# Splitting a weight unit over three chunks of time, and copying out the second accumulator ahead of the rounding

## The chip, the cores and the metric

The kernel runs on one core of a Trainium2 chip. Its time is the device time of one execution in microseconds (us). TensorE (PE in the profile; PEld is its weight load) multiplies matrices into PSUM, VectorE (DVE) and ScalarE (ACT) work elementwise on SBUF and PSUM, GpSimd (POOL) works on SBUF alone, and SyncE (SP) issues the transfers. Each engine runs its own queue in order; what crosses engines is ordered by semaphores.

## The reference

A 7-tap convolution with weights made from a softmax at every token, and two two-layer networks one after the other, on 8192 tokens of 192 values with 2048 hidden values:

```python
w = softmax(weight_gen)                     # per token and head, over 7 taps
x = einsum('bshk,bskhg->bshg', w, x_unf)    # x_unf: the last 7 tokens, 8 heads of 24
h = x @ w_in                                # 192 -> 2048
g = where(h > 0, h, exp(minimum(h, 0)) - 1)
x = g @ w_out                               # 2048 -> 192
h = x @ w_in2
g = h * clip(h + 3, 0, 6) / 6
out = g @ w_out2
```

## The kernel before

**Precision.** TensorE takes rounded 32-bit operands (F32R) at its fast rate. To come near full precision, every operand of a product is kept as a high part (rounded) and a low part (the rest), and a product is three matmuls: high by high, high by low, low by high. So x is split into `xh` and `xl`, g into `gh` and `gl`, and each weight into `_h` and `_l` tiles.

**Blocks, chunks, units.** The tokens come in 16 blocks of 512 (`NB`). A *chunk* is one block with 256 of the 2048 hidden values: 18 matmuls to make h (`first_product`, two halves k of 64 partitions that run as pairs, in the banks h), the nonlinearity, and, three chunks later (`LAG`), 20 matmuls of g with `w_out` (`second_product`) into two accumulators, `acca` and `accb`. In the order of the list `cells`, chunks 0 to 15 (`BOOT`, `EARLY`) serve blocks 0 and 1 with the first network's weights as they arrive, five slices of block 0, five of block 1, and the rest; from chunk 16 each block takes 8 chunks in a row, 128 chunks for each network. A *unit* is a slice of 384 columns of a weight (`w_in` or `w_out`) that has to be split into its parts. Units 0 to 15 are the first network's; chunk d needs its unit split before it starts.

**Splitting a unit.** It is loaded as 64-bit words (`raw`). ScalarE takes an absolute value (L150), VectorE does five steps (`s0` to `s4`: L154, L157, L161, L169, L178), ScalarE casts the high part (L171, queued in `s3`, and ready to run when L161 is done). For units 0 to 15, TensorE then adds up the low part in PSUM (`p5`: L183 to L185, the "low product"), and ScalarE casts it out (`p6`: L190, the "low cast"). The working tile of the five steps is a PSUM bank for units flagged `busy`, and the SBUF tile `bootf` for the others.

**The order.** It is written out by hand. In chunk n, TensorE gets `matmuls(n)` and then the low product of the unit whose steps were queued at the end of chunk n-1 (`at[u] == n - 1`). ScalarE and VectorE get `act_a` and `gate` of half 1 and of half 0 (two activations, L487 and L488, and the VectorE operation L504, the "gate"), the low cast, then `round_g` (ScalarE casts gh of chunk n-1, L494, the "rounding") and `rest_g` (VectorE makes gl, L498). At the chunk's end ScalarE's absolute value and VectorE's five steps of the next unit are queued, with ScalarE's high cast. From chunk 16 on, the rounding stands between the two halves of activations.

**Around it.** GpSimd makes the convolution's products of a block (L278 to L299); they wait for the softmax weights (VectorE, L268) and for the tile `y`, of which there is one. `prepare` transposes y on TensorE (L323, L327), casts `xh` on ScalarE (L334), makes `xl` on VectorE (L336) and moves halves of both by transfers, which for blocks 1 and 2 wait for the next chunk (`later(1, ...)`). When a block's last second product is done, `fold_b` copies `accb` to SBUF (L359), or, for blocks 0 and 1, whose sums were begun earlier, adds the kept part to it on VectorE (L357); a chunk later `fold_a` copies `acca`, and ScalarE (L364) and VectorE (L366) put the two together as z. The next block's first matmul into `accb` waits for this.

Of the kernel before, what the change touches and what calls it, by code (L numbers as in the profile page):

```python
# [17 lines left out]
def kernel(  # L18
# [105 lines left out]
    class Unit:  # L124
# [39 lines left out]
        def s3(self):  # L164
            if self.m == 0 and self.busy:
                self.r = self.b
            else:
                self.r = stage.tile([P, UN], U32, tag="tr", name="tr", bufs=2)
            nc.vector.tensor_scalar(self.r, self.f, 0xFF800000, None, op0=ALU.bitwise_and)  # L169
            hi, _, v = self.parts()  # L170
            nc.scalar.copy(hi, v(self.f.bitcast(F32)))  # L171
# [139 lines left out]
    def prepare(m, i, parts=(0, 1)):  # L311
# [20 lines left out]
        def split():  # L332
# [6 lines left out]
            for k in "hl":  # L339
                for a in range(2):  # L340
                    later(1 if first[m, i] <= BOOT else 2, X[k][half[1 - a], 1].bitcast(F32), X[k][half[a], 0].bitcast(F32))
# [7 lines left out]
    def fold_b(m, i):  # L349
# [6 lines left out]
        if (m, i) in part:  # L356
            nc.vector.tensor_tensor(b, accb, part.pop((m, i)), op=ALU.add)  # L357
        else:
            nc.scalar.copy(b, accb)  # L359
        bv, zb = b.rearrange("p (h t c) -> p h t c", h=2, c=HP), v[:, :, TM:]  # L360

        def rest():
            for k in range(2):
                nc.scalar.copy(zb[half[k]], bv[half[1 - k], :, 2 * k:2 * k + 2])  # L364
# [207 lines left out]

    at = []
    for d, *_ in units:
        at.append(min(d - 2, at[-1] + 1) if at else -2)
# [8 lines left out]
    def want(n):  # L584
        if n < len(units) and n not in made:
            u = made[n] = Unit(*units[n])
            u.n = n
            if n < BOOT:
                u.busy = at[n] < 3 or at[n] > 7
# [16 lines left out]
    begin = {i: max(8, prep[0, i - 1] + (i == 3)) for i in range(2, NB)}  # L606
# [4 lines left out]
    with tc.manual_schedule():  # L611
# [11 lines left out]
        for s in todo["a"] + todo["w"]:  # L623
            s()
        made[0].p5()
# [5 lines left out]
        for s in c1[4:] + w_steps(1):  # L631
            s()
        wst = Stream(wtasks)
        for n in range(len(cells) + LAG + 3):
            now = n
            jobs = []
            for m, i in order:
# [4 lines left out]
                elif (m, i) == (0, 2) and 0 <= n - prep[m, i] < 2:  # L642
                    jobs.append(prepare(m, i, (n - prep[m, i],)))
# [3 lines left out]
            low = [made[u] for u in range(BOOT) if at[u] == n - 1]  # L647
            for u in low:
                u.p5()

            for k in (1, 0):
                if n < len(cells):
                    act_a(n, k)
                    gate(n, k)
                if not k:
                    for u in low:
                        u.p6()
                if k == (n >= BOOT) and 1 <= n <= len(cells):
                    round_g(n - 1)
                    rest_g(n - 1)  # L660
                if not k:
                    continue
                if n - LAG in (SPLIT - 1, 2 * SPLIT - 1):
                    keep_b(*ends[n - LAG])
                for b in order:
                    if n == last[b] + LAG:
                        fold_b(*b)
# [55 lines left out]
```

## Time and profile before

| | |
|---|---|
| median of 3 runs | 1295.91 us (1294.05 to 1296.14) |
| profiled execution | 1292.77 us, span 1291.0 us |
| TensorE busy | 1215.9 us (94%) |
| VectorE busy | 940.5 us (73%) |
| ScalarE busy | 852.5 us (66%) |
| GpSimd busy | 411.1 us (32%) |

A share of busy time is an average over stretches with different limits. The kernel has a first part, in which weights and x arrive and are split while chunks 0 to 15 run, and a long even part. The profile's views used here give busy time by stretch with the granted TensorE clock (1.00 is 2.4 GHz, and the other level is half of it), who waited for whom, and the instructions of an engine in order of time, with the idle time ahead of one and what ended it in brackets.

### The profile page before, as it was taken

Reading aid. Unit: us, or ns where it says so; the run is one execution under the profiler, and the core shown is the slowest. Engines: PE = TensorE matmul, PEld = TensorE weight load, DVE = VectorE, ACT = ScalarE, POOL = GpSimd, SP = SyncE. Lnnn points to the kernel's source line nnn. Section 1 sums busy time; section 2 is a strip of 40 time slices with the busy share of each in tenths; the row PEclk is TensorE's granted clock in tenths of the full one; section 3 lists DMA queues with packets and bytes.
Section 4 is the critical chain, followed back from the end, with each engine's and each line's share of the span. In section 5 each row is a group of like instructions: output and inputs, shape, how many; then the busy total and the mean of one; then the engine's idle time right before and its main releaser. Section 6 shows DMA issues by size and latency. Waiting matters only on the chain.

```text
span 1291.0 us, 25448 instructions
## 1 busy us (share of the span) xinstructions
PE 1215.9 (94%) x10176; PEld 1093.0 (85%) x10176; DVE 940.5 (73%) x1226; ACT 852.5 (66%) x1340; POOL 411.1 (32%) x234
## 2 busy tenths in 40 slices
PE   3777779999999999999999999999999999999998
PEld 2555658888888988888887799999999999999996
DVE  5778478898888988988876766666666666666663
ACT  2554457788878887888887556665555665656653
POOL 7434258766666887666500000000000000000000
PEclk9888889999999999999999999999999999999999
DMA  6231112222112222221121111111111111111110
GB/s 175 74 108 37 48 50 84 84 85 66 53 50 84 84 85 84 80 66 36 38 62 50 38 51 50 36 34 44 50 50 51 43 45 50 50 32 31 50 39 25
DMA packets 33686, 75.82 MB, mean 59 GB/s; under 512 B 4644, under 2 KB 17058, under 8 KB 33568
## 3 DMA queue, kind: packets, MB, share of 16 engines
q1 hardware_dynamic: 33568, 74.19, 19.8%
q8 instruction: 80, 1.31, 0.4%
q14 instruction: 38, 0.31, 0.1%
HBM read 36.43 MB, written 12.58 MB: 38 GB/s over the span
## 4 chain that ended last, share of the span: by engine, by line
PE 67%; ACT 15%; DVE 13%; issue 3%; DMA 1%; SPq 0%; DVEq 0%; ACTq 0%
PE h L467 30%; PE acca L467 21%; PE accb L467 14%; DVE gl L498 5%; ACT gh L494 4%; ACT r L487 4%; ACT r L488 4%; DVE r L504 2%; DMA xl<-xl 1%; DVE tr L169 1%; DVE bootf L161 1%; DVE wt L243 1%; DVE aux L157 1%; DMA xt<-in_x_dram 1%; ACT fold L359 0%
## 5 line engine op out<-in xcount | busy, mean ns | idle before, releaser
L467 PE MATMUL h<-xh,wi_h 64*128 64x512 f32 x1536 | 581.8, 400 | 5.0 <-DVE xl L336 2.6
L467 PE MATMUL h<-xh,wi_l 64*128 64x512 f32 x1536 | 583.6, 400 | 0.1
L467 PE MATMUL h<-xl,wi_h 64*128 64x512 f32 x1536 | 573.5, 397 | 2.7 <-DMA xl<-xl 2.0
L498 DVE TENSOR_TENSOR gl<-r,gh 128x1024 fp32r<-128x1024 f32 x256 | 372.6, 1456 | 64.3 <-ACT gh L494 63.0
L490 ACT ACTIVATE r<-h,three 128x512 f32<-128x512 f32 x256 | 176.2, 688 | 229.9 <-PE h L467 117.0
L467 PEld LDWEIGHTS h<-xh,wi_h 64*128 64x128 f32 x1536 | 288.6, 188 | 19.9 <-DMA xh<-xh 3.1
L507 DVE SCALAR_TENSOR_TENSOR r<-r,h 128x512 f32<-128x512 f32 x256 | 176.0, 688 | 173.9 <-ACT r L490 173.1
L467 PEld LDWEIGHTS h<-xl,wi_h 64*128 64x128 f32 x1536 | 285.7, 187 | 17.8 <-DMA xl<-xl 3.0
L467 PEld LDWEIGHTS h<-xh,wi_l 64*128 64x128 f32 x1536 | 285.6, 187 | 14.7 <-ACT wi_l L190 0.9
L467 PE MATMUL acca<-gh,wo 64*128 64x512 f32 x1024 | 286.7, 400 | 0.0
L494 ACT CAST gh<-r 128x1024 fp32r<-128x1024 f32 x256 | 265.9, 1039 | 2.1 <-DVE r L504 1.3
L504 DVE SCALAR_TENSOR_TENSOR r<-r,h 128x512 f32<-128x512 f32 x256 | 174.4, 682 | 84.4 <-ACT r L488 84.0
L467 PEld LDWEIGHTS acca<-gh,wo 64*128 64x128 f32 x1024 | 193.7, 189 | 15.3
L487 ACT ACTIVATE r<-h 128x512 f32<-128x512 f32 x256 | 152.5, 596 | 79.1 <-PE h L467 48.6
L278 POOL TENSOR_TENSOR tmp<-xt,wt 128x768 f32<-128x768 f32 (+1 forms) x96 | 190.0, 1979 | 7.0 <-DMA xt<-in_x_dram 0.8
L467 PE MATMUL accb<-gh,wo 64*128 64x512 f32 x512 | 170.8, 414 | 15.5 <-ACT fold L359 6.0
L488 ACT ACTIVATE r<-r 128x512 f32<-128x512 f32 x256 | 162.0, 633 | 8.1
L467 PE MATMUL accb<-gl,wo 64*128 64x512 f32 x512 | 165.9, 404 | 0.0
L467 PE MATMUL acca<-gl,wo 64*128 64x512 f32 x512 | 163.2, 399 | 0.0
L285 POOL TENSOR_TENSOR y<-y,tmp 128x768 f32<-128x768 f32 (+1 forms) x80 | 146.6, 1832 | 6.3
L467 PE MATMUL acca<-gh,wo1b 64*128 64x512 f32 x512 | 140.9, 394 | 0.3
L467 PE MATMUL acca<-gh,wo1a 64*128 64x512 f32 x512 | 140.3, 393 | 0.0
(143 smaller groups left out, 1850.4 us busy)
## 6 DMA issues: line engine op xcount, KB each, us to landing
xt<-in_x_dram SPq DMA_DIRECT2D x14, 960.0 KB, 5.4
xh<-xh SPq DMA_DIRECT2D x64, 192.0 KB, 2.7
xl<-xl SPq DMA_DIRECT2D x64, 192.0 KB, 2.9
raw<-in_moe_w_out_dram SPq DMA_DIRECT2D x16, 384.0 KB, 3.2
z<-z SPq DMA_DIRECT2D x16, 384.0 KB, 2.3
zin<-z SPq DMA_DIRECT2D x16, 384.0 KB, 3.0
out_dram<-ot SPq DMA_DIRECT2D x16, 384.0 KB, 2.3
raw<-in_moe_w_in_dram SPq DMA_DIRECT2D x16, 192.0 KB, 3.4
```

The source lines that it names most:

```text
L157: nc.vector.tensor_scalar(self.b, self.b, 3, 0x3FFFFFF8, op0=ALU.logical_shift_left, op1=ALU.bitwise_and)
L161: nc.vector.scalar_tensor_tensor(self.f, self.hw, 0xC0000000, self.b, op0=ALU.bitwise_and, op1=ALU.bitwise_or)
L278: eng.tensor_tensor(o.rearrange("p t (h g) -> p t h g", g=G), xk, wk.rearrange("p (t h) g -> p t h g", h=H), op=ALU.mult)
L285: eng.tensor_tensor(y[:, t, :], y[:, t, :], o, op=ALU.add)
L467: mm = nc.tensor.matmul(o, w, r, start=st, stop=sp).ins
L487: nc.scalar.activation(r, h, AF.Relu, scale=-1.0)
L488: nc.scalar.activation(r, r, AF.Exp, scale=-1.0)
L490: nc.scalar.activation(r, h, AF.Relu, bias=three)
L494: nc.scalar.copy(gg[n][0], rs[n])
L498: nc.vector.tensor_tensor(gl, rs.pop(n), gh.bitcast(F32), op=ALU.subtract)
L504: nc.vector.scalar_tensor_tensor(r, r, -1.0, h, op0=ALU.add, op1=ALU.max)
L507: nc.vector.scalar_tensor_tensor(r, r, 6.0, h, op0=ALU.min, op1=ALU.mult)
```

## The change

Units 0 to 15 have their stages apart. In chunk n, TensorE does the low product of the unit whose five steps were queued at the end of chunk n-2, and ScalarE its low cast; the high cast, now a function of its own (`high`), is queued at the start of chunk n for the unit of chunk n-1. All units are begun one chunk earlier (`d - 3` for `d - 2`), and unit 2 before chunk 0. `busy` is now set for units 0 to 5 alone, so units 6 to 15 do their five steps in SBUF; before, that were units 7 to 11. For chunks before 16, rounding and `rest_g` of chunk n-1 come at the start of chunk n, ahead of the activations. Block 2 is begun one chunk later (`max(9, ...)`), its two transposes stand ahead of the chunk's activations (`early`), and its transfers go out in the same chunk. From chunk 16 on, the copy of the second accumulator stands ahead of the rounding; for blocks 0 and 1 it is a copy on ScalarE too, and the kept part is added a chunk later on VectorE, from SBUF.

```diff
             nc.vector.tensor_scalar(self.r, self.f, 0xFF800000, None, op0=ALU.bitwise_and)
+            if self.m:
+                self.high()
+
+        def high(self):
             hi, _, v = self.parts()
             nc.scalar.copy(hi, v(self.f.bitcast(F32)))
...
-                    later(1 if first[m, i] <= BOOT else 2, X[k][half[1 - a], 1].bitcast(F32), X[k][half[a], 0].bitcast(F32))
+                    later(first[m, i] == SPLIT if first[m, i] <= BOOT else 2, X[k][half[1 - a], 1].bitcast(F32), X[k][half[a], 0].bitcast(F32))
...
         if (m, i) in part:
-            nc.vector.tensor_tensor(b, accb, part.pop((m, i)), op=ALU.add)
-        else:
-            nc.scalar.copy(b, accb)
+            first_part = part.pop((m, i))
+        else:
+            first_part = None
+        nc.scalar.copy(b, accb)
...
         def rest():
+            if first_part is not None:
+                nc.vector.tensor_tensor(b, b, first_part, op=ALU.add)
...
-        at.append(min(d - 2, at[-1] + 1) if at else -2)
+        at.append(min(d - 3, at[-1] + 1) if at else -3)
...
-                u.busy = at[n] < 3 or at[n] > 7
+                u.busy = n < 6
...
-    begin = {i: max(8, prep[0, i - 1] + (i == 3)) for i in range(2, NB)}
+    begin = {i: max(9, prep[0, i - 1] + (i == 3)) for i in range(2, NB)}
...
+        made[1].high()
+        for s in w_steps(2):
+            s()
...
-                    jobs.append(prepare(m, i, (n - prep[m, i],)))
+                    early = prepare(m, i, (n - prep[m, i],))
...
-            low = [made[u] for u in range(BOOT) if at[u] == n - 1]
+            low = [made[u] for u in range(BOOT) if at[u] == n - 2]
             for u in low:
                 u.p5()
+            if early:
+                early()
+            if 1 <= n < BOOT:
+                round_g(n - 1)
+                rest_g(n - 1)
+            for u in range(BOOT):
+                if at[u] == n - 1:
+                    made[u].high()
...
+                if k:
+                    if n - LAG in (SPLIT - 1, 2 * SPLIT - 1):
+                        keep_b(*ends[n - LAG])
+                    for b in order:
+                        if n == last[b] + LAG:
+                            fold_b(*b)
+                if k and BOOT <= n <= len(cells):
+                    round_g(n - 1)
+                    rest_g(n - 1)
                 if not k:
                     for u in low:
                         u.p6()
-                if k == (n >= BOOT) and 1 <= n <= len(cells):
-                    round_g(n - 1)
-                    rest_g(n - 1)
```

Where this puts things shows in the queues. On ScalarE, chunk 6 before: absolute value (L150) and high cast (L171) of unit 9, the activations, unit 9's low casts (L190, a `w_out` unit has two), and the rounding of chunk 5's g (L494).

```order
L150 ACTIVATE bootf<-raw 128x384
L171 CAST wo_88<-bootf 128x2x192
L487 ACTIVATE r<-h_73 128x512
L488 ACTIVATE r<-r 128x512
L487 ACTIVATE r<-h_72 128x512
L488 ACTIVATE r<-r 128x512
L190 CAST wo_88<-aux 128x2x128
L190 CAST wo_88<-aux 128x2x64
L494 CAST gh<-r 128x1024
```

The same chunk on ScalarE in the changed kernel, whose line numbers are 4 to 7 higher (L175, L194, L494, L495 and L501 are the operations above):

```order
L150 ACTIVATE bootf<-raw 128x384
L501 CAST gh<-r 128x1024
L175 CAST wi_h<-bootf 128x384
L494 ACTIVATE r<-h_73 128x512
L495 ACTIVATE r<-r 128x512
L494 ACTIVATE r<-h_72 128x512
L495 ACTIVATE r<-r 128x512
L194 CAST wo_88<-aux 128x2x128
L194 CAST wo_88<-aux 128x2x64
```

The absolute value and the high cast are now those of unit 10, a `w_in` unit, while the low casts are still unit 9's; and the rounding moved from the end to the front. On VectorE, before, the last softmax product of block 2 (L268, on which GpSimd waits) stands at the end of chunk 6, and unit 10's five steps behind it:

```order
L498 TENSOR_TENSOR gl<-r,gh 128x1024
L268 TENSOR_TENSOR wt<-wt,mx 128x224
L154 TENSOR_SCALAR bootf<-bootf 128x384
L157 TENSOR_SCALAR bootf<-bootf 128x384
L161 SCALAR_TENSOR_TENSOR bootf<-raw,bootf 128x384
L169 TENSOR_SCALAR tr<-bootf 128x384
L178 SCALAR_TENSOR_TENSOR bootr<-raw,tr 128x384
L504 SCALAR_TENSOR_TENSOR r<-r,h_75 128x512
```

In the changed kernel the same product (L272) stands at the end of chunk 7, behind that chunk's gates (L511):

```order
L511 SCALAR_TENSOR_TENSOR r<-r,h_74 128x512
L272 TENSOR_TENSOR wt<-wt,mx 128x224
L154 TENSOR_SCALAR bootf<-bootf 128x384
L157 TENSOR_SCALAR bootf<-bootf 128x384
L161 SCALAR_TENSOR_TENSOR bootf<-raw,bootf 128x384
L169 TENSOR_SCALAR tr<-bootf 128x384
L182 SCALAR_TENSOR_TENSOR bootr<-raw,tr 128x384
L505 TENSOR_TENSOR gl<-r,gh 128x1024
```

The five steps are now unit 12's, and gl comes behind them. On ScalarE again, chunks 15 and 16 in the changed kernel, where block 0's sum is copied out (L364, absent there before):

```order
L501 CAST gh<-r 128x1024
L494 ACTIVATE r<-h_75 128x512
L495 ACTIVATE r<-r 128x512
L364 COPY fold<-accb 128x512
L494 ACTIVATE r<-h_74 128x512
L495 ACTIVATE r<-r 128x512
L494 ACTIVATE r<-h_73 128x512
L495 ACTIVATE r<-r 128x512
L501 CAST gh<-r 128x1024
L378 COPY z<-acca_76 128x2x256
L371 COPY z<-fold 64x2x128 x2
```

The copies of z (L371) now wait for VectorE's addition of the kept part (L369), which stands there one chunk later than the old one (L357).

## Rows read from the trace of the kernel before

**Rows 1.** Busy time by stretch: us and (instructions) of each engine, granted clock, DMA.

```profile
23.31:59.53 36.22, 28.71 (x127) 19.28 (x129) 23.66 (x40) 19.39 (x38) 21.94 (x14) 0.86 0.43 126
59.53:83.25 23.72, 19.46 (x133) 14.55 (x129) 16.27 (x31) 14.71 (x31) 0.00 (x0) 0.93 0.30 78
83.25:140.83 57.58, 42.19 (x256) 29.83 (x257) 46.10 (x55) 29.40 (x55) 24.55 (x14) 0.84 0.24 75
140.83:164.37 23.54, 18.81 (x128) 17.32 (x128) 9.35 (x12) 9.20 (x16) 11.23 (x7) 0.82 0.00 1
164.37:204.80 40.43, 32.20 (x243) 25.99 (x244) 28.94 (x39) 25.44 (x42) 22.02 (x13) 0.87 0.18 54
204.80:646.00 441.20, 434.42 (x3764) 381.82 (x3762) 391.85 (x488) 358.62 (x582) 314.91 (x164) 1.00 0.23 70
```

**Rows 2.** TensorE in order of time, chunks 6 to 8: start, us, instruction, [idle before].

```profile
75.67 0.50 PE L467 MATMUL accb<-gh,wo 64*128 64x512 f32 x1 [0.63 <-ACT wo L190]
...
79.99 0.39 PE L467 MATMUL h<-xh,wi_l 64*128 64x512 f32 x1
...
81.24 0.33 PE L185 MATMUL aux<-bootr,plus 128*128 128x384 f32 x1
...
94.48 0.62 PE L467 MATMUL accb<-gh,wo 64*128 64x512 f32 x1
```

**Rows 3.** Who waited for whom: us in total, times, longest us.

```profile
PE accb L467 <- ACT fold L359: 6.0, 11, 0.6
PE accb L467 <- DVE fold L357: 4.6, 1, 4.6
PE h L467 <- DMA xh<-xh: 2.4, 1, 2.4
```

**Rows 4.** ScalarE in order of time, chunk 6.

```profile
79.95 0.52 ACT L171 CAST wo<-bootf 128x384 fp32r<-128x384 f32 x1 [2.94 <-DVE bootf L161]
...
80.37 0.59 ACT L487 ACTIVATE r<-h 128x512 f32<-128x512 f32 x1
...
82.68 0.52 ACT L190 CAST wo<-aux 128x256 fp32r<-128x256 f32 x2
...
83.09 1.06 ACT L494 CAST gh<-r 128x1024 fp32r<-128x1024 f32 x1
```

**Rows 5.** GpSimd in order of time, blocks 1 and 2.

```profile
39.78 2.66 POOL L285 TENSOR_TENSOR y<-y,tmp 128x768 f32<-128x768 f32 x1
...
85.93 1.54 POOL L278 TENSOR_TENSOR y<-xt,wt 128x768 f32<-128x768 f32 x1 [39.81 <-PE acca L467]
...
109.63 1.71 POOL L299 TENSOR_TENSOR y<-y,tmp 128x256 f32<-128x256 f32 x1
```

**Rows 6.** VectorE in order of time, units 9 and 11, and blocks' sums.

```profile
78.63 0.30 DVE L154 TENSOR_SCALAR bootf<-bootf 128x384 f32<-128x384 f32 x1
...
80.35 0.56 DVE L178 SCALAR_TENSOR_TENSOR bootr<-raw,tr 128x384 fp32r<-128x384 uint32 x1
...
95.45 2.15 DVE L498 TENSOR_TENSOR gl<-r,gh 128x1024 fp32r<-128x1024 f32 x1 [1.04 <-ACT gh L494]
...
97.53 1.99 DVE L154 TENSOR_SCALAR bootf<-bootf 128x384 f32<-128x384 f32 x1
...
104.86 2.05 DVE L178 SCALAR_TENSOR_TENSOR bootr<-raw,tr 128x384 fp32r<-128x384 uint32 x1
...
163.62 0.68 DVE L357 TENSOR_TENSOR fold<-accb,bootf 128x512 f32<-128x512 f32 x1
...
174.61 3.20 DVE L366 TENSOR_TENSOR z<-fold,z 64x256 f32<-64x256 f32 x2
```

**Rows 7.** Block 1's second x transfers: issue; and, by issue, KB, us to landing.

```profile
65.55 1.24 SPq L546 DMA_DIRECT2D xl<-xl  x2
...
xl<-xl SPq DMA_DIRECT2D x2, 192.0 KB, 3.3
```

**Rows 8.** The page's costliest groups: the gate; busy, mean ns of one, idle before.

```profile
L504 DVE SCALAR_TENSOR_TENSOR r<-r,h 128x512 f32<-128x512 f32 x256 | 174.4, 682 | 84.4 <-ACT r L488 84.0
```

More of the change, by code (lines that the diff above doesn't have):

```diff
@@ L624 @@
             s()
+        made[0].high()
         made[0].p5()
@@ L635 @@
             now = n
-            jobs = []
+            jobs, early = [], None
             for m, i in order:
@@ L657 @@
                         u.p6()
-                if k == (n >= BOOT) and 1 <= n <= len(cells):
-                    round_g(n - 1)
-                    rest_g(n - 1)
                 if not k:
                     continue
[L663 to L667, printed above, removed]
                 for b in order:
```

## The prediction, made before the changed kernel was run

> **What bounds the kernel now.** I began with the busy time by stretch, cut at the starts of chunks 0, 4, 7, 13, 16 and 22 [rows 1]. From chunk 22 on TensorE is the bound (434.42 of 441.20 us in the first part, at the full clock); before, it is not. The five stretches from 23.31 to 204.80 us hold 22 chunks in 181.5 us, 8.25 us a chunk, though 19 matmul pairs cost little over half of that: pairs follow each other every 0.234 us, the first restarts slower, and chunk 6 runs from 75.67 to the end of its last matmul at 80.38, 4.71 us [rows 2]. No other engine is full in those stretches, and the granted clock is 0.82 to 0.93. So the loss is waiting in rings of engines, and I looked next at what TensorE waits for [rows 3]: weights not split in time, a copy of the second accumulator, x transfers. The ScalarE order shows how a ring closes [rows 4]: in chunk 6 its high cast starts at 79.95 after 2.94 us of waiting for VectorE, so the activations, whose matmuls are nearly done, start at 80.37, the low casts end at 83.2, and chunk 7 starts at 83.25 [rows 1].
>
> **The change, stretch by stretch.** The sum is made against the profiled execution, 1292.77 us with a span of 1291.0.
>
> *Chunks 0 to 3 (36.22 us).* Unit 2 is split before chunk 0, in VectorE's idle time, and units 3 and 4 are ready when TensorE wants them, where it waited before. But chunk 3 needs the low casts of units 3 and 4, which now stand behind the high casts of units 5 and 6 on ScalarE. Unit 6 works from SBUF, at about 40 to 47 us, while GpSimd is still at block 1 (an instruction of it took 2.66 us at 39.78 [rows 5]). Worked forward from chunk 0, whose rows the change leaves alone: VectorE ends the ten steps of units 3 and 4 at 37.2 us, gl and the gates of chunk 1 at 40.3; of unit 6's steps the third is the one the cast needs, and with 1.5 us of GpSimd ahead of each it ends at 45.2; high cast 0.5, four activations 2.35, low casts 0.9 make the start of chunk 3 49.0 us. It runs at the low clock, as it did, and I put chunk 4 half a microsecond early: **-0.5** (bounds -4, if unit 6 isn't held up, to +3).
>
> *Chunks 4 to 6 (23.72 us, 7.9 each).* The low casts of a chunk still gate the next one here, so the ring is now TensorE, the last two activations, the low casts: 4.71 + 1.2 + 0.55 + 0.1 for hand-overs = 6.6 us. VectorE's part (0.7 for the last gate, 1.4 for three steps of the split, which run 78.63 to 80.91 for all five [rows 6], 0.45 for the high cast) falls into the first 2.5 us of a chunk, before its first activation can start, and is hidden. Three chunks are 19.8. A new wait comes with it: the x transfers of block 1 still go out late in chunk 4; the second tensor's first one was issued at 65.55, 6.0 us after the chunk's start, and takes 3.3 us to land [rows 7]. Landing is 9.3 us after chunk 4's start, and chunk 5, starting at 6.6, wants it at its fifth pair, at 7.7: 1.6 us lost. 21.4 against 23.72: **-2.3** (bounds -4 to 0).
>
> *Chunks 7 to 12 (57.58 us).* Units 10 to 15 are now due three to five chunks after they are made, so low casts gate nothing. Left are 4.71 for the matmuls and 1.25 for the low product behind them (from 80.38 to 81.57 [rows 2]), 5.95 a chunk, 35.7 for six. ScalarE's work, 29.40 us for the six [rows 1], fits under this. Not under it is the collision with GpSimd. In the trace, block 2's products hold GpSimd from 85.93 to 111.3 [rows 5], and the five steps of the second unit in that time take from 97.53 to 106.9, 9.4 us in place of 2.3; all five read and write SBUF [rows 6]. The change starts block 2 one chunk later, and units 12 to 15, whose steps worked in PSUM, now work in SBUF. The 25 us therefore land on units 12 and 13, as they landed on 10 and 11. From the start of chunk 8, VectorE: 1.0 softmax product, 7.5 unit 12 (its first step is ahead of GpSimd), 2.1 the low part of g (2.15 at 95.45 [rows 6]), 1.3 two gates (0.68 each [rows 8]) = 11.9; then 9.3 for unit 13 = 21.2. TensorE reaches unit 13's low product after three chunks less one low product, 3 x 5.95 - 1.25 = 16.6, and waits 4.7. It then restarts at the low clock (+1.5), waits 0.9 for the gates of chunk 9 and 1.0 for the low casts ahead of unit 14: 8.1 in all. 43.8 against 57.58: **-13.8** (bounds -20, nothing collides on the path, to -4, units 14 and 15 collide too).
>
> *Chunks 13 to 15 (23.54 us).* No unit is left. Block 2's transposes come in chunks 13 and 14, with their casts now ahead of the rounding on ScalarE; behind those casts wait the rounding and both activations. TensorE: 4.7 + 0.6, 4.7 + 0.6, 4.7 = 15.3. But ScalarE, from the end of chunk 14's transposes (10.4): cast 0.4, rounding 0.95, four activations 2.35 (80.37 to 82.68 [rows 4]), gate 0.7, rounding 0.95, two activations 1.2, accumulator copy 0.6 = 17.5, and chunk 16 needs that copy. 17.5 against 23.54: **-6.0** (bounds -8 to -3).
>
> *Chunks 16 to 21 (40.43 us).* The x transfers of block 2 go out a chunk sooner; their waits (2.4 of [rows 3] and the smaller ones) and the low clock behind them go, about 5.7 of the 40.43. Against that, the addition of the first accumulator part, once on VectorE out of PSUM (0.68 at 163.62, beside a working GpSimd), is now an SBUF addition, and ScalarE's copies of z stand behind it, with activations queued after them. The two SBUF additions at 174.61 took 3.2 us together beside GpSimd [rows 6], so I take 1.5 for it. I get 2.8 us of late gates in chunk 18. The wait for the second accumulator's copy before chunk 19, 4.6 in [rows 3], loses about 2 us by the copy's new place and gets them back from VectorE being later: 4.3, plus 1.7 at the low clock. Six chunks at 4.45 are 26.7; with 8.8 of waits 35.5: **-4.9** (bounds -11 to +3).
> The Trainium skill ("SBUF — State Buffer", Who interferes with whom) says that a VectorE instruction with two SBUF inputs waits for the whole GpSimd instruction that reads SBUF, which speaks against this edit. By it the addition costs the 1.5 taken; by the PSUM row alone it would cost 0.7, and the sum would be 0.8 us better.
>
> *Chunk 22 on.* The copy before the rounding is 0.95 us sooner. It ended up to 0.6 us late, 11 times, 6.0 us in all [rows 3]: **-6.0** (bounds -6 to -4; the rounding is 0.6 later once in eight chunks, and its reader is two chunks away).
>
> Sum: -0.5 - 2.3 - 13.8 - 6.0 - 4.9 - 6.0 = -33.5, so 1259.3 for the profiled execution. The runs shown have their median 3.1 us above it; on their footing the forecast is **1262 us**, 2.6% faster.
>
> **The rivals.** (1) *The collision spreads.* Each VectorE step holds GpSimd up as well, so block 2 lasts longer and units 14 and 15 are hit: 7 us each, nearly all on the path: 1276. For it: the SBUF form from unit 6 on. Against: 12 slow steps filled GpSimd's 25 us in the trace, and two units with their g bring as many. (2) *The late stalls vanish*: the copy's new place takes all of the 4.3 + 1.7 + 2.8 of chunks 18 and 19: 1253. For it: the copy stands ahead of rounding and VectorE. Against: a high cast that waits for VectorE stands ahead of the copy. (3) *The stages aren't apart on ScalarE.* High casts stand in front of the activations as before; if VectorE delivers them late in every chunk, chunks 4 to 12 keep about 7.6 us: 2 and 10 us of the gain go, 1274. Against: gate, three steps, cast and four activations make 5.0 us, less than the 5.95 of TensorE. (4) *Slower: TensorE stays at 1.2 GHz.* At the low clock a matmul takes 0.62 us, as at 94.48, in place of 0.39 [rows 2], and pairs come every 0.43 us: 8.6 us a chunk in place of 4.7, and 0.9 more where there is a low product. If the short idle times between waits kept the clock down in the nine chunks that TensorE bounds (4 to 8, 12 to 15), that is about 4.5 x 9 = 41 us: 1303. It turns the sign when 8 of the 9 run so. Against: chunk 6 ran at full pace after a wait, and the stretch of chunks 4 to 6 had a granted clock of 0.93 with 19.46 of 23.72 us busy.
> The Trainium skill ("TensorE: Matmul & The Clock Gate", Why this matters for your kernels) wants matmuls kept dense for the clock to hold; by it the denser chunks here should gain clock, and rival 4 gets little.
>
> **How the numbers follow.** Forecast 50% (1250 to 1270), rival 1 20%, rival 2 14%, rival 3 11%, rival 4 5%. Taking half of each stretch's bounds together gives 1248 to 1280; that holds the forecast and rivals 1 to 3, and leaves out rival 4 and the ends. About 0.2% (2.6 us) is what a measurement of this kernel can tell from no change. Faster by more: 94%; within: 2%; slower: 4%.
>
> **What would show it.** Chunk starts near 59, 80, 124, 141 and 177 us in place of 59.53, 83.25, 140.83, 164.37 and 204.80. ScalarE's high cast in chunks 4 to 8 without idle time that delays an activation. VectorE's slow SBUF steps on units 12 and 13, and one TensorE wait of some 5 us for unit 13 or its low casts. No wait for the accumulator copy after chunk 22. I am wrong if slow steps show on units 14 and 15, if the high cast still waits in every chunk, if the matmuls of chunks 4 to 8 run at 0.43 us, or if chunk 3 starts after 52 us.

## The result, and the profile after

| | before | after |
|---|---|---|
| median of 3 runs | 1295.91 us | 1260.29 us (1259.71 to 1260.44) |
| profiled execution: span | 1291.0 us | 1258.7 us |

The ratio is 0.9728, with a 95% interval of 0.9706 to 0.975. The forecast was 1262 us. It came within 2 us, but not because each term was right: the largest was wrong by 4.1 us, and two others made up for most of it.

First the busy time by stretch, cut at the same chunks as in [rows 1] (starts of chunks 0, 4, 7, 13, 16 and 22; the last line runs to the end). Columns as there: us and (instructions) of PE, PEld, DVE, ACT and POOL, granted clock, DMA share, GB/s.

```profile
23.74:57.90 34.16, 31.48 (x127) 21.76 (x129) 27.83 (x46) 21.53 (x40) 22.30 (x14) 1.00 0.48 142
57.90:79.42 21.52, 18.43 (x136) 13.48 (x130) 15.37 (x28) 15.65 (x31) 0.00 (x0) 1.00 0.33 81
79.42:127.29 47.87, 39.98 (x257) 28.13 (x258) 43.77 (x54) 28.01 (x52) 24.66 (x14) 0.89 0.26 85
127.29:144.56 17.27, 16.27 (x130) 14.37 (x128) 8.35 (x11) 10.52 (x17) 10.21 (x6) 0.90 0.19 52
144.56:180.52 35.96, 31.27 (x243) 24.40 (x244) 30.84 (x37) 23.83 (x41) 24.23 (x14) 0.91 0.12 38
180.52:1258.70 1078.18, 1069.43 (x9288) 971.39 (x9284) 800.45 (x1019) 752.23 (x1151) 315.62 (x164) 1.00 0.19 55
```

The clock column reads 1.00 in the first line although single matmuls take 0.62 us there until about 45.8 us, as at 1.2 GHz: it missed the low clock of chunks 0 to 2, and this entry is not to be set beside the 0.86 of [rows 1].

Against the forecast, in us:

| chunks | before | forecast | after | gain forecast | gain measured |
|---|---|---|---|---|---|
| 0 to 3 | 36.22 | 35.7 | 34.16 | 0.5 | 2.1 |
| 4 to 6 | 23.72 | 21.4 | 21.52 | 2.3 | 2.2 |
| 7 to 12 | 57.58 | 43.8 | 47.87 | 13.8 | 9.7 |
| 13 to 15 | 23.54 | 17.5 | 17.27 | 6.0 | 6.3 |
| 16 to 21 | 40.43 | 35.5 | 35.96 | 4.9 | 4.5 |
| 22 to the end | 1086.2 | 1080.2 | 1078.18 | 6.0 | 8.0 |

The gains measured sum to 32.7; chunk 0 starts 0.43 us later than before (23.74 for 23.31), which leaves the 32.3 us between the spans.

What TensorE waits for has changed. Lines of the view of waits (us in total, times, longest us) answer [rows 3]: the eleven waits for the copy of the accumulator are one, the addition is gone from the list, and new names have come.

```profile
PE aux L327 <- ACT wo L194: 3.4, 2, 3.0
PE aux L187 <- ACT wi_l L194: 3.3, 1, 3.3
PE h L474 <- DVE r L511: 3.2, 4, 1.2
PE accb L474 <- ACT fold L364: 2.5, 1, 2.5
PE h L474 <- DMA xl<-xl: 2.0, 2, 1.2
PE accb L474 <- SPq L478: 1.0, 1, 1.0
```

**Chunks 7 to 12.** Chunks 7 to 9 take 5.83 us each: the stages are apart, and TensorE is the bound. Then GpSimd's products of block 2 begin at 86.91 us. VectorE in order of time, units 12 and 13 (the last row is of unit 14):

```profile
86.60 0.36 DVE L154 TENSOR_SCALAR bootf<-bootf 128x384 f32<-128x384 f32 x1
86.99 1.67 DVE L157 TENSOR_SCALAR bootf<-bootf 128x384 uint32<-128x384 uint32 x1
...
94.14 2.87 DVE L505 TENSOR_TENSOR gl<-r,gh 128x1024 fp32r<-128x1024 f32 x1
...
106.00 2.83 DVE L505 TENSOR_TENSOR gl<-r,gh 128x1024 fp32r<-128x1024 f32 x1
...
112.68 0.36 DVE L157 TENSOR_SCALAR bootf<-bootf 128x384 uint32<-128x384 uint32 x1
```

The first step of unit 12 is 0.36 us, the next beside GpSimd 1.67; after GpSimd's last instruction the same step of unit 14 is 0.36 again. TensorE in the same stretch:

```profile
105.65 1.65 PE L187 MATMUL aux<-bootf,ident 128*128 128x384 f32 x2 [3.28 <-ACT wi_l L194]
...
109.48 0.79 PE L474 MATMUL h<-xh,wi_h 64*128 64x512 f32 x1 [0.82 <-DVE r L511]
...
113.06 0.62 PE L474 MATMUL accb<-gh,wo 64*128 64x512 f32 x1
...
116.97 0.91 PE L187 MATMUL aux<-bootf,ident 128*128 128x384 f32 x2 [0.55 <-ACT wo L194]
...
127.07 0.43 PE L327 MATMUL aux<-ident,y 64*128 64x64 f32 x4 [2.99 <-ACT wo L194]
```

The wait for unit 13 is there (3.28 us; the forecast had 4.7), the late gates (0.82 for 0.9), and the low cast (0.55 for 1.0). But after the first wait TensorE runs at 1.2 GHz until 114.6 us (0.62 us a matmul), and ahead of chunk 13 stands a wait of 2.99 us that the forecast didn't have.

What ended the 3.28 us was not VectorE itself but a low cast on ScalarE, that of unit 12, which had to leave the bank `aux` before unit 13's low product could use it. ScalarE in order of time:

```profile
102.41 0.51 ACT L175 CAST wo<-bootf 128x384 fp32r<-128x384 f32 x1 [3.12 <-DVE bootf L161]
...
105.13 0.46 ACT L194 CAST wi_l<-aux 128x384 fp32r<-128x384 f32 x1
```

The low cast stands behind the activations of chunk 9, and these behind the high cast of unit 13, which waited 3.12 us for VectorE's third step. So inside the collision the old ring through ScalarE is closed again. VectorE's fifth step of unit 13 ended only at 106.07 us (104.29 and 1.78), and the low product needs that too, so the slow steps are the root either way.

### The profile page after: what moved, and what is told of

Its sections match the earlier page's. It is cut to its first block, busy times and chain, and to the rows that moved or that the text cites. A ratio compares the mean times of both kernels' runs of the same rounds, so it can differ in the third digit from the quotient of the medians.

```text
span 1258.7 us, 25471 instructions
## 1 busy us (share of the span) xinstructions
PE 1210.0 (96%) x10176; PEld 1075.4 (85%) x10176; DVE 941.3 (75%) x1226; ACT 857.1 (68%) x1342; POOL 413.5 (33%) x234
## 4 chain that ended last, share of the span: by engine, by line
PE 90%; DVE 5%; ACT 3%; DMA 1%; issue 1%; SPq 0%; DVEq 0%; ACTq 0%
PE h L474 41%; PE acca L474 28%; PE accb L474 19%; DVE gl L505 1%; ACT r L495 1%; ACT r L494 1%; DVE bootf L161 1%; DVE r L511 1%; DMA xt<-in_x_dram 1%; DMA xl<-xl 0%; DVE bootf L157 0%; DVE tr L169 0%; PE acca L327 0%; SPq L544 0%; DVE z L373 0%
## 5 line engine op out<-in xcount | busy, mean ns | idle before, releaser
L474 PE MATMUL h<-xh,wi_h 64*128 64x512 f32 x1536 | 574.2, 399 | 5.9 <-DVE r L511 3.2
L474 PE MATMUL h<-xh,wi_l 64*128 64x512 f32 x1536 | 574.8, 399 | 0.0
L474 PE MATMUL h<-xl,wi_h 64*128 64x512 f32 x1536 | 567.7, 398 | 2.0 <-DMA xl<-xl 2.0
L501 ACT CAST gh<-r 128x1024 fp32r<-128x1024 f32 x256 | 266.6, 1041 | 13.2 <-DVE r L511 12.4
L511 DVE SCALAR_TENSOR_TENSOR r<-r,h 128x512 f32<-128x512 f32 x256 | 174.1, 682 | 55.3 <-ACT r L495 54.6
L494 ACT ACTIVATE r<-h 128x512 f32<-128x512 f32 x256 | 152.7, 596 | 50.6 <-PE acca L474 26.9
L474 PE MATMUL accb<-gh,wo 64*128 64x512 f32 x512 | 165.6, 402 | 6.9 <-ACT wo L194 3.4
L495 ACT ACTIVATE r<-r 128x512 f32<-128x512 f32 x256 | 162.3, 634 | 8.1
L474 PE MATMUL accb<-gl,wo 64*128 64x512 f32 x512 | 163.0, 398 | 0.0
L289 POOL TENSOR_TENSOR y<-y,tmp 128x768 f32<-128x768 f32 (+1 forms) x80 | 149.9, 1874 | 6.3
```

Of the source, the lines that this page charges most:

```text
L289: eng.tensor_tensor(y[:, t, :], y[:, t, :], o, op=ALU.add)
L474: mm = nc.tensor.matmul(o, w, r, start=st, stop=sp).ins
L494: nc.scalar.activation(r, h, AF.Relu, scale=-1.0)
L495: nc.scalar.activation(r, r, AF.Exp, scale=-1.0)
L501: nc.scalar.copy(gg[n][0], rs[n])
L511: nc.vector.scalar_tensor_tensor(r, r, -1.0, h, op0=ALU.add, op1=ALU.max)
```

## The experiments

Times are medians of 4 runs, each kernel beside runs of the kernel before on its own chip (1293.63, 1295.44 and 1294.50 us for the three groups). Where I compare stretches, the start of half 0's first activation in a chunk serves as the mark, and chunks a to b run from the mark of chunk a-1 to that of chunk b.

Two cautions on small differences. The kernel before took 1293.63 to 1295.91 us in the four groups of runs, so a difference of under some 2 us between a kernel here and the changed kernel tells nothing. And each kernel has one trace, in which chunk 3 can be about 2 us and a stop in the second network 1.55 us dearer or not, without any edit touching them (both are told below).

**1. What is a late copy worth?** The fold copy goes back behind the rounding.

```diff
-                    for b in order:
-                        if n == last[b] + LAG:
-                            fold_b(*b)
                 if k and BOOT <= n <= len(cells):
                     round_g(n - 1)
                     rest_g(n - 1)
+                if k:
+                    for b in order:
+                        if n == last[b] + LAG:
+                            fold_b(*b)
```

> The changed kernel with one thing undone: the copy of the second accumulator stands behind the rounding on ScalarE again, in all blocks. Theory 1, now that the two traces are compared: a late copy costs more than its idle time. The distance between the kernels grows by 0.85 us a block from chunk 22 on where the trace of before showed 0.55 to 0.58 us of idle time; so this kernel loses 0.85 x 12 = 10.2 us there and about 1 us in chunk 18, 1270 to 1272 us. Theory 2, as the forecast had it: the idle time alone, 6.0 us, so 1266 to 1267 us. If the copy's place doesn't matter at all: 1260 us.

1271.47 us, 0.983 of before (0.9807 to 0.9853), so 11.2 us slower than the changed kernel (13 us, when each is set against the kernel before on its own chip). Theory 1 holds. TensorE in order of time at the start of a block, kernel before:

```profile
263.66 0.40 PE L467 MATMUL acca<-gl,wo 64*128 64x512 f32 x1
264.63 0.49 PE L467 MATMUL accb<-gh,wo 64*128 64x512 f32 x1 [0.58 <-ACT fold L359]
...
264.97 0.39 PE L467 MATMUL accb<-gh,wo 64*128 64x512 f32 x1
```

and the same place in the changed kernel:

```profile
239.00 0.39 PE L474 MATMUL acca<-gl,wo 64*128 64x512 f32 x1
239.21 0.39 PE L474 MATMUL accb<-gh,wo 64*128 64x512 f32 x1
...
239.44 0.39 PE L474 MATMUL accb<-gh,wo 64*128 64x512 f32 x1
```

Pairs start every 0.234 us. With the late copy the starts are 0.97 and then 0.34 us apart: 0.74 + 0.11 = 0.85 us are lost, while the idle column says 0.58, since it counts from the end of the last matmul, 0.40 us after its start, and not from the start that the next pair would have had. Eleven of them make 9.4 us. By the marks, chunks 23 to 127 take 484.88 us with the late copy and 475.04 in the changed kernel, 9.8 us apart; two later copies add a little (0.35 and 0.23 us) that shows in no wait.

**2. The fold edit alone**, in the kernel before: accumulator copies ahead of the rounding, the kept part added from SBUF, nothing else.

```diff
...
+                if k:
+                    if n - LAG in (SPLIT - 1, 2 * SPLIT - 1):
+                        keep_b(*ends[n - LAG])
+                    for b in order:
+                        if n == last[b] + LAG:
+                            fold_b(*b)
                 if k == (n >= BOOT) and 1 <= n <= len(cells):
                     round_g(n - 1)
...
```

> The kernel before with the second part of the change alone: accumulator copies ahead of the rounding, and the kept part added in SBUF; the stages of units as they were. If the parts add up and a late copy costs 0.85 us a block: 1295.9 - 10.4 = 1285.5 us, plus or minus 2 for chunks 16 to 21, where the addition in SBUF can hold VectorE up and the copy can come sooner. By the forecast's term for the copies (6.0 us): 1290 us. What is left between this kernel and the changed one, about 25 us, is then the stages and the transfers.

1283.52 us, 0.9925 (0.9904 to 0.9946): 10.1 us less than before on the same chip. Of the change's 35.6 us about 10 are this part; the other 25 are the stages and what was moved with them. By the marks the 10 lie from chunk 23 on: chunks 23 to 127 take 474.95 us, as in the changed kernel, and 485.18 before; chunks 15 to 22 take 52.15 for 50.89. The 25 were not taken apart further: no run undoes by itself the high cast's new place, the earlier start of the units or the rounding at the front, so how much each of them gives stays open.

**3. and 4. What is the collision worth, and what makes it?** In the first kernel ten of GpSimd's fourteen instructions for block 2 are left out, so a part of the convolution isn't computed.

```diff
-        for k in range(K - 2, -1, -1):
+        for k in range(K - 2, -1, -1) if i != 2 else (0,):
```

> The changed kernel with ten of GpSimd's fourteen instructions for block 2 left out (the products of the five inner taps and their sums; some 18 of 25 us). It leaves out a part of the computation. Theory: units 12 and 13 are slow only because GpSimd works beside VectorE. Then most of their slow steps go, chunks 10 and 11 come near the 5.83 us of chunks 7 to 9 (they took 11.0 and 10.2), chunk 13 starts 7 to 10 us sooner, 1250 to 1253 us. The wait of 3.0 us ahead of chunk 13, for the low cast of unit 15, stays, for it has nothing to do with GpSimd. Rival: TensorE's waits in chunks 10 and 11 come from the ring of stages itself: no change, 1260 us.

In the second, GpSimd does all of its work, and units 12 to 15 take their steps in the PSUM bank `aux`.

```diff
-                u.busy = n < 6
+                u.busy = n < 6 or n > 11
```

> The changed kernel with the steps of units 12 to 15 in the PSUM bank aux again (the shift, the clamp and the exponent word are there, the other operands stay in SBUF), GpSimd complete. Theory 1: a VectorE step is slow beside GpSimd when all that it reads and writes is in SBUF; the steps of units 12 and 13 fall from 1.7 to 1.9 us to some 0.4 to 0.7, gl stays slow (2.8), chunks 10 and 11 take 6 to 7 us, 1251 to 1254 us. Theory 2: any VectorE instruction is slowed beside a working GpSimd: 1260 us. Theory 3: aux, which now serves the steps of one unit and the low product of the one before it in turn, becomes a ring: TensorE waits ahead of each low product for the last step of the next unit, 0.5 to 1.5 us in four chunks, and 1255 to 1262 us come out of it.

Without most of GpSimd's work 1247.79 us (0.964, 0.9624 to 0.9656), 12.5 us less than the changed kernel, and 2 us below the theory's range. Chunks 7 to 12 there, by stretch up to the transposes, and the wait ahead of them:

```profile
80.47:116.66 36.19, 35.27 (x252) 25.56 (x253) 31.91 (x53) 28.05 (x52) 5.46 (x4) 1.00 0.28 90
```

```profile
116.66 0.43 PE L327 MATMUL aux<-ident,y 64*128 64x64 f32 x4 [0.92 <-ACT wo L194]
```

TensorE is busy for all but that 0.92 us, at the full clock. In the changed kernel the stretch up to the transposes is 127.07 - 79.42 = 47.65 us: the collision is worth 11.5 us, and 2.07 of the 2.99 us ahead of chunk 13 belong to it. This term of the expectation was wrong: the wait did not stay.

With the steps in PSUM 1251.61 us (0.9669, 0.9654 to 0.9685), inside the range of theory 1. VectorE, unit 13, with GpSimd at work from 88.96 us on:

```profile
94.31 0.57 DVE L154 TENSOR_SCALAR aux<-aux 128x384 f32<-128x384 f32 x1
...
95.51 0.56 DVE L161 SCALAR_TENSOR_TENSOR bootf<-raw,aux 128x384 uint32<-128x384 uint32 x1
...
97.17 2.26 DVE L505 TENSOR_TENSOR gl<-r,gh 128x1024 fp32r<-128x1024 f32 x1
```

The steps take 0.55 to 0.57 us where the same steps all in SBUF took 1.67 to 1.89; gl, all in SBUF still, takes 2.26 (1.22 alone). So it isn't GpSimd beside VectorE that costs, but GpSimd beside a `tensor_scalar`, `scalar_tensor_tensor` or `tensor_tensor` of the sizes above that works in SBUF alone. Not every SBUF instruction is slowed: in the changed kernel the softmax's `tensor_reduce` (128x224, L246 and L254) took 0.37 to 0.39 us each time, beside GpSimd too. The price of PSUM is small: 0.57 for 0.36 us when nothing collides. Theory 2 falls. One wait of 2.03 us for a unit's last step is left of theory 3.

**5. Block 2 one chunk sooner**, as before the change.

```diff
-    begin = {i: max(9, prep[0, i - 1] + (i == 3)) for i in range(2, NB)}
+    begin = {i: max(8, prep[0, i - 1] + (i == 3)) for i in range(2, NB)}
```

> The changed kernel with one thing undone: GpSimd's products of block 2 start in chunk 8 in place of 9, as before the change. They then meet units 11 and 12 in place of 12 and 13. Theory 1: the collision costs the same there (11.5 us of chunks 7 to 12, from the kernel with little GpSimd work), but the last unit has a chunk more to catch up, so of the wait of 2.99 us ahead of chunk 13 only the 0.92 us stay that the kernel without collision shows: 1257 to 1259 us. Theory 2: the collision's price doesn't depend on its place and the wait ahead of chunk 13 is just handed on: 1260 to 1261 us. Theory 3: units 11 and 12 are nearer to their chunks than 12 and 13: 1262 us and more.

1260.44 us (0.9734, 0.9719 to 0.9748): theory 2. The collision meets units 11 and 12 (and two steps of unit 13), TensorE waits 2.36 and 2.17 us there (3.28, 0.82 and 0.55 in the changed kernel), and 2.80 us still ahead of chunk 13, 20 us after GpSimd's last instruction. So the delay is handed on from the collision to the next place where TensorE needs a cast; that ScalarE doesn't catch up with a TensorE that takes 4.7 to 5.8 us a chunk is the likely reason, and wasn't tried by itself. By these medians the new start of block 2 neither gains nor loses.

**6. The x transfers.** Block 2's go out a chunk later again:

```diff
-                    later(first[m, i] == SPLIT if first[m, i] <= BOOT else 2, X[k][half[1 - a], 1].bitcast(F32), X[k][half[a], 0].bitcast(F32))
+                    later(1 if first[m, i] <= BOOT else 2, X[k][half[1 - a], 1].bitcast(F32), X[k][half[a], 0].bitcast(F32))
```

> The changed kernel with one thing undone: the x transfers of block 2 go out a chunk later again. The forecast put their waits and the low clock behind them at 5.7 us in chunks 16 to 21. Theory 1: they are issued at about 143 to 145 us in place of 138.55 to 141.0 and chunk 16, which starts by 143 us, waits for them: 4 to 6 us, 1264 to 1266 us. Theory 2: chunk 16 now starts sooner against the transposes than in the kernel before, so the waits are longer, 6 to 9 us: 1266 to 1269 us. Theory 3: chunk 16 is held by the accumulator copy (144.5 us) and the gates anyway: 1260 to 1262 us.

1263.9 us (0.9755, 0.9733 to 0.9777): 3.6 us by the medians, between theories 1 and 3. The trace is of the quickest of the four runs (1260.40 us; the others took 1263.57 to 1264.64), and in it chunks 14 to 23 take 58.45 us for 55.92, so 2.5 us are shown by stretch; it had no loss at the stop in the second network. TensorE in order of time:

```profile
145.33 0.79 PE L474 MATMUL h<-xh,wi_h 64*128 64x512 f32 x1 [2.27 <-DMA xh<-xh]
147.08 0.79 PE L474 MATMUL h<-xl,wi_h 64*128 64x512 f32 x1 [0.95 <-DMA xl<-xl]
...
166.76 0.49 PE L474 MATMUL accb<-gh,wo 64*128 64x512 f32 x1 [3.69 <-ACT fold L364]
```

The waits of the kernel before are back, 3.2 us and the restarts behind them, but the wait for SyncE (below) is gone, and the wait ahead of chunk 19 is longer (3.69 for 2.53). The other way, with block 1's transfers issued in their own chunk too, `later(0 if first[m, i] <= BOOT else 2, ...)`:

> The changed kernel with the x transfers of block 1 issued in their own chunk (3), in place of the end of chunk 4. Theory 1: the wait of 1.20 us for xl in chunk 5 and the slower restart behind it go, so chunk 5 takes 6.55 us in place of 8.41: 1258 to 1259 us. Theory 2: SyncE's notes, by which one half of TensorE's matmuls waits for the other, stand behind the four issues, as at 141.07 us, where TensorE waits 1.00 us for SyncE; 1 to 2 us are lost in chunk 4: 1260 to 1261 us.

1268.03 us (0.9797, 0.9781 to 0.9813), 7.7 us slower: theory 2, at several times its price. In the trace chunk 4 takes 14.54 us for 7.85 and chunk 5 7.04 for 8.23, so the transfers cost 5.5 us; another 2.2 are chunk 3 at the low clock, ahead of them. TensorE in chunk 4:

```profile
65.74 0.79 PE L474 MATMUL accb<-gh,wo 64*128 64x512 f32 x1 [4.20 <-SPq L478]
```

What TensorE waits for is a note on SyncE (L478), by which one half of the matmuls learns that the other half is done with the accumulator. SyncE works in order. It issues the x transfers from 60.55 us on, then four weight loads up to 65.6, and only then the notes. In the changed kernel the same happens once, after block 2's transfers (139.79 to 140.96 us):

```profile
141.07 0.50 PE L474 MATMUL accb<-gh,wo 64*128 64x512 f32 x1 [1.00 <-SPq L478]
```

The chunk of delay for block 1 is what keeps its transfers from holding the notes up.

**7. Chunks 16 to 21.** In the changed kernel a chain runs through ScalarE and VectorE. ScalarE in order of time:

```profile
152.88 0.83 ACT L371 COPY z<-fold 64x256 f32<-64x256 f32 x2 [3.68 <-DVE fold L369]
...
162.93 0.48 ACT L175 CAST wi_h<-aux 128x384 fp32r<-128x384 f32 x1 [3.46 <-DVE tr L169]
...
164.48 0.57 ACT L364 COPY fold<-accb 128x512 f32<-128x512 f32 x1
```

VectorE's addition of the kept part, beside a working GpSimd and, the second time, begun just ahead of GpSimd's next work (171.89 us):

```profile
150.51 2.33 DVE L369 TENSOR_TENSOR fold<-fold,bootf 128x512 f32<-128x512 f32 x1
...
171.43 0.69 DVE L369 TENSOR_TENSOR fold<-fold,bootf 128x512 f32<-128x512 f32 x1
```

and TensorE, which pays:

```profile
157.29 0.50 PE L474 MATMUL h<-xh,wi_h 64*128 64x512 f32 x1 [1.22 <-DVE r L511]
158.95 0.79 PE L474 MATMUL h<-xh,wi_h 64*128 64x512 f32 x1 [0.93 <-DVE r L511]
...
165.10 0.50 PE L474 MATMUL accb<-gh,wo 64*128 64x512 f32 x1 [2.53 <-ACT fold L364]
```

Three kernels each take one link out. First the addition, again straight out of PSUM, at the new place:

```diff
-            first_part = part.pop((m, i))
-        else:
-            first_part = None
-        nc.scalar.copy(b, accb)
+            nc.vector.tensor_tensor(b, accb, part.pop((m, i)), op=ALU.add)
+        else:
+            nc.scalar.copy(b, accb)
...
-            if first_part is not None:
-                nc.vector.tensor_tensor(b, b, first_part, op=ALU.add)
```

> The changed kernel with the form of one addition undone: for blocks 0 and 1 VectorE again adds the kept part straight out of the PSUM bank accb, at the new place ahead of the rounding, and ScalarE doesn't copy accb there. Theory 1: the SBUF addition (2.33 us at 150.51 us beside GpSimd) is what ScalarE's z copies wait for (3.68 us idle ahead of 152.88 us), and the late gates of chunk 18 (TensorE waits 1.22 and 0.93 us) follow from it; out of PSUM it takes 0.7 us and stands a chunk earlier, so about 2 to 4 us are gained: 1256 to 1258 us. Theory 2: ahead of chunk 19 VectorE is later than ScalarE with freeing accb (the kernel before waited 4.61 us there, the changed one 2.53 us), and what is gained in chunk 18 is lost in chunk 19: 1259 to 1261 us.

1260.76 us (0.9739, 0.972 to 0.9757): theory 2. TensorE's 1.22 us in chunk 18 go (the 0.93 stay), and the activations of that part are 3 us sooner (150.70 for 153.73 us), but chunk 19 takes it back:

```profile
165.40 0.76 PE L471 MATMUL accb<-gh,wo 64*128 64x512 f32 x1 [4.96 <-ACT r L491]
```

In that kernel VectorE's addition frees the accumulator, from 164.57 to 165.25 us, and it stands behind a gate whose activation stands behind the high cast of unit 16. (The profile names the activation that ended at 165.36, a tenth later, in the same queue behind that cast.) Second, that cast: unit 16 begun in chunk 20 (its loads issued as before).

```diff
-        wtasks.append([max(BOOT, c - 3), c + (3 if n < NB - 2 else 2 if n % 2 else 6)])
+        wtasks.append([max(BOOT + 4, c - 3), c + (7 if n == 0 else 3 if n < NB - 2 else 2 if n % 2 else 6)])
...
+            if n == BOOT:
+                for a in range(3):
+                    want(BOOT + a)
```

> The changed kernel with the steps of unit 16, the first of the second network, begun in chunk 20 in place of chunk 16 (its loads go out as they did). Theory 1, the forecast's reason against its second rival: the high cast of unit 16 waits on ScalarE for VectorE's third step (3.46 us idle ahead of 162.93 us) and stands ahead of the accumulator copy that chunk 19 needs (TensorE waits 2.53 us at 165.10, then runs at the low clock to 169 us). Without it the copy comes 3 us sooner: 3 to 5 us gained, 1255 to 1257 us. Theory 2: the activations of chunk 18 are late for another reason, VectorE's sums of z and gates, and the copy is as late as before: 1259 to 1261 us.

1260.89 us (0.9734, 0.9712 to 0.9757). Both theories are half right. Chunks 14 to 21 take 45.39 in place of 47.81 us, and the wait ahead of chunk 19 falls to 1.14; then chunks 22 on lose more than that:

```profile
187.29 0.50 PE L474 MATMUL h<-xh,wi_h 64*128 64x512 f32 x1 [1.72 <-DVE r L511]
...
204.66 0.49 PE L474 MATMUL accb<-gh,wo 64*128 64x512 f32 x1 [1.87 <-ACT fold L364]
```

Unit 16's steps now share chunks 20 to 26 with those of unit 17, beside GpSimd again, which is the likely reason. Third, unit 16 begun in chunk 14, where no unit is split, with units 12 to 15 in PSUM:

```diff
-        wtasks.append([max(BOOT, c - 3), c + (3 if n < NB - 2 else 2 if n % 2 else 6)])
+        wtasks.append([max(BOOT - 2, c - 3), c + (1 if n == 0 else 3 if n < NB - 2 else 2 if n % 2 else 6)])
...
-                u.busy = n < 6
+                u.busy = n < 6 or n > 11
```

> The kernel with units 12 to 15 in PSUM (1251.6 us) and unit 16 begun in chunk 14, where no other unit is split, in place of chunk 16. Begun in chunk 20 it took 2.4 us out of chunks 14 to 21 and gave them back from chunk 22 on, where its steps stood beside those of unit 17. Theory 1: in chunks 14 to 16 nothing is given back: the wait ahead of chunk 19 (4.01 us in the kernel with units in PSUM) shrinks, 1248 to 1250 us. Theory 2: ScalarE's chain sets the length of chunks 13 to 15, and its two more instructions and the high cast's wait for VectorE stand in it: 1 to 3 us lost there, 1250 to 1253 us.

1251.53 us (0.9669, 0.9654 to 0.9683), the same as without: in theory 2's range, but not for its reason. No wait is left ahead of chunk 19; the late gates of chunk 18 cost more (2.43 us for 1.20), and unit 16's step brings weight loads, which at that time go to SyncE at once, and they stand ahead of the notes:

```profile
136.37 0.49 PE L474 MATMUL accb<-gh,wo 64*128 64x512 f32 x1 [3.63 <-SPq L478]
```

**8. Combinations.** The first has units 12 to 15 in PSUM, the addition out of PSUM, unit 16 in chunk 20, and unit 15's low cast ahead of chunk 12's activations; the second is the kernel of psum_u16 with block 1's transfers in their own chunk.

> Four edits of the changed kernel together: units 12 to 15 in PSUM (1251.6 us by itself), the kept part added out of PSUM, unit 16 begun in chunk 20, and the low cast of unit 15 ahead of the activations of chunk 12 (0.92 us of waiting ahead of chunk 13 in the kernel with units in PSUM). If the gains add up: 1251.6 - 3 - 4 - 0.9 = 1243 to 1245 us. If the addition out of PSUM gives nothing: 1246 to 1248 us.

> The kernel of the run before with the x transfers of block 1 in their own chunk. If both gains hold (1.8 us in chunk 5): 1246 to 1248 us. If the notes on SyncE take the gain: as without, 1248 to 1250 us.

The first gave 1254.86 us (0.969, 0.9652 to 0.9728) and is not settled: two of its four runs took 1250.4 and 1250.9 us, two 1258.9 and 1259.0, at a mean clock of 0.994 to 0.998 and of 0.987. Only one of the quicker ones has a trace, so what the others lost is open. The second gave 1256.59 us (0.9703, 0.9685 to 0.9722); its transfers cost 5 us by the medians, by the same wait (4.17 us for SyncE). Gains didn't add up in either. The best version that I can vouch for is the changed kernel with units 12 to 15 in PSUM, 1251.6 us.

## Why the prediction was right, and where it was not

**Chunks 0 to 3** (0.5 forecast, 2.1 measured). The start of chunk 3 was right to a microsecond: 50.03 us, or 49.6 when the trace's later start is taken off, for 49.0, but only in part for the reason given. Unit 6 beside GpSimd cost less than put down: two of its steps took 1.23 and 1.17 us, and its third ended 3.9 us after the gates of chunk 1, for 4.9. VectorE came to it later than worked out: units 3 and 4 ended at 38.7 us for 37.2, and with gl at 2.57 us beside GpSimd the gates ended at 42.4 for 40.3. These errors offset each other. What was mis-sized is the clock behind it. The forecast had chunk 3 at the low clock. In this execution it ran at 2.4 GHz, 6.85 us from the mark of chunk 2 to that of chunk 3; in seven of the other eleven kernels that have the change's stages it took 8.4 to 9.3 us. So these 2 us can't be credited to the change.

**Chunks 4 to 6** (2.3 and 2.2). Right term by term: chunks of 6.57 and 6.54 us (forecast 6.6), and the new wait for `xl` in chunk 5, 1.20 us (1.6).

**Chunks 7 to 12** (13.8 and 9.7). The mechanism was right: units 12 and 13, ten slow VectorE instructions in GpSimd's 25.5 us, one long wait for unit 13, no spread to units 14 and 15. The size was not: 8.1 us put down, 11.5 measured by taking GpSimd's work out. Two steps failed. The restart at the low clock was put at 1.5 us; the low product and most of chunk 11 ran at 1.2 GHz, 9 us in all. Chunk 11 without its two waits took 8.9 us, where chunks 7 to 9 took 5.83, so about 3.1 were lost there and 1.0 in the low product. And the transposes of block 2 share `aux` with unit 15's low cast; the forecast counted that cast as gating nothing. It costs 0.92 us without a collision and 2.99 with one. And the wait for unit 13 (4.7 us forecast, 4.6 by its own terms, 3.28 measured) was ended by unit 12's low cast on ScalarE, a queue that the forecast had left out there.
The Trainium skill ("SBUF — State Buffer", Who interferes with whom) says that a VectorE instruction with at most one SBUF input does not contend with GpSimd outside the modes that use both ports, and that `tensor_scalar` can enter these. The runs agree with both halves: `tensor_scalar` in SBUF took 1.67 us beside GpSimd and 0.36 alone, and in PSUM 0.57 beside it. The forecast had used this page for the addition alone.

**Chunks 13 to 15** (6.0 and 6.3). The number was right, the reason only in part. The forecast let ScalarE's chain set the time. In the trace ScalarE waits for TensorE ahead of the last activations of chunk 15 (1.47 us), because TensorE had waited 1.00 us for SyncE's note behind the transfers and had run at the low clock from 128.1 to 131.7 us. The transfers' issue on SyncE was a queue that the forecast didn't walk through. (Its 17.5 also starts from 10.4 us for the end of chunk 14's transposes, where its own terms give 10.6.)

**Chunks 16 to 21** (4.9 and 4.5). Right in sum and close in the terms: late gates 2.15 us (2.8), the wait ahead of chunk 19 2.53 (4.3), the addition 2.33 (1.5 taken), and more low clock than put down: 14 pairs at 0.43 us for 0.234, 2.7 us (1.7). The transfers were too dear: 5.7 us of the stretch were laid to them, undoing them costs 2.5 in the trace and 3.6 by the medians. The second rival, that these stalls vanish, was turned down for a reason that holds in the main: the high cast that waits for VectorE stands ahead of the copy, and without it the wait ahead of chunk 19 falls from 2.53 to 1.14. The three experiments on this stretch show why its sum is hard to move: each link taken out of the ring lets the next one, or SyncE, wait as long.

**Chunk 22 on** (6.0 and 8.0). The step that failed took the idle column for the loss. It is 0.85 us a copy, not 0.55: 9.4 us. The forecast knew the spacing of 0.234 us and the slower restart and didn't use them. Of the 9.4, 1.5 were lost again to the clock at 707.53 us (below).

The rivals: the collision didn't spread to units 14 and 15; the stages are apart on ScalarE in chunks 7 to 9 (5.83 us a chunk), though not inside the collision, where the third rival's high cast did hold the activations up; and TensorE didn't stay at 1.2 GHz: the granted clock of chunks 4 to 6 rose from 0.93 to 1.00. That 4.1 us too much in chunks 7 to 12 met 2.0 and 1.6 us too little at the end and the beginning is luck; the range of 1248 to 1280 us allowed for it. That range is wider than its rule: half of each stretch's bounds together gives about 1252 to 1276, in which the result lies too.

## What to carry to other kernels

Cost a wait of a pipelined engine by the distance of its starts, not by the idle time that the profile prints, and add the slower restart. When VectorE steps move from PSUM to SBUF, look for GpSimd beside them: the form that is quicker alone (0.36 for 0.57 us) can be three times slower there. And when a transfer or a load is moved, walk the issuing queue too: what stands behind it may be a semaphore that another engine needs.

## What was not expected of the hardware

The same idle time doesn't always have the same consequence for TensorE's clock. In every trace of this study TensorE stands still once for 2.0 to 2.1 us early in the second network, put down to issue, with the same work around it. In the changed kernel:

```profile
707.53 0.47 PE L474 MATMUL accb<-gh,wo1b 64*128 64x512 f32 x1 [2.06 <-issue]
...
709.52 0.62 PE L474 MATMUL acca<-gh,wo1b 64*128 64x512 f32 x1
```

In the kernel before:

```profile
741.43 0.47 PE L467 MATMUL accb<-gh,wo1b 64*128 64x512 f32 x1 [2.08 <-issue]
...
743.13 0.39 PE L467 MATMUL acca<-gh,wo1b 64*128 64x512 f32 x1
```

After the stop the first runs at 1.2 GHz for 3.3 us and loses 1.55 us; the second stays at 2.4 GHz. Of the fourteen kernels with a trace four lost these 1.55 us and ten did not. With the 2 us of chunk 3 that makes some 3.6 us by which these traces differ at places that no edit touches; a smaller difference in the whole of two traces shouldn't be put down to an edit.
